# Loads of tokens in halves, and of logits, each issued once a crossbar transpose has landed

## The chip, the cores and the metric

One core of one Trainium2 chip. The metric is the device time of one execution in microseconds (us). An execution also has a span, from its first to its last instruction, which is 1.75 us shorter, and a mean granted clock of TensorE. In the profile PE is TensorE (PEld its weight loads), DVE is VectorE, ACT is ScalarE, POOL is GpSimd, SP is SyncE; a `q` behind one of them is its sequencer.

With one core there are no two dies to compare. An execution is called slow here only if it took over 1.5% more than the fastest of the same kernel.

## The reference, cut to what matters

```python
# x: (8, 4160, 192), weight_gen: (8, 4160, 8 heads, 7 taps), float32
w = softmax(weight_gen, axis=-1)                  # over the taps
out = einsum('bshk,bskhg->bshg', w, last_7_rows_of(x))   # each row and the 6 before it
x = out.reshape(33280, 192)
g = maximum(x @ w1, x @ w2)                       # 192 -> 1024
return g @ w_out                                  # 1024 -> 192
```

## The kernel before

A partition holds 260 consecutive tokens, its *columns*. They go through in batches of 16 columns, and a batch in *units* of 8 (4 at the start and the end). For each unit VectorE multiplies and adds (`mul`, `adds`), the result `y` is turned round by a crossbar transpose, a DMA issued by SyncE, and TensorE reads the transposed tile `yt`. Units are counted from 0; unit 6 is the second half of batch 1 and the second to be transposed by DMA.

```python
def load_x(b, o, n):                     # GpSimd's queue, float32 -> bfloat16 on the way
    ...
    nc.gpsimd.dma_start(out=xb_ts[b][:, (PAD + o) * D:(PAD + o + n) * D], in_=x[...])
    if b > 0 and o == 0:                 # the "halo": the last 6 rows of the batch before
        nc.gpsimd.dma_start(out=xb_ts[b][:, 0:PAD * D],
                            in_=xb_ts[b - 1][:, 16 * D:(16 + PAD) * D])

def transpose(u):
    b, o, n = UNITS[u]
    yt = pyt.tile([P, 8 // 2 * 3 * P], BF16, name="yt", tag="yt")          # 6 buffers
    nc.sync.dma_start_transpose(out=yt[...], in_=y_ts[b][:, o * D:(o + n) * D])
    yt_ts[u] = yt

def rest_of_1():
    shift(2); mul(1, 8)
    load_wg(5, nc.gpsimd)                # logits of batch 5
    load_x(3, 0, 16)                     # x of batch 3, whole
    adds(1, 8)

def extra(t):                            # beside tile t (one tile a column)
    u, k = TILES[t]; b, o, n = UNITS[u]; s = o + k
    ...
    if s == 3 and b + 2 < NB:
        if b + 5 < NB: load_wg(b + 5, nc.gpsimd)
        if b + 3 < NB: load_x(b + 3, 0, BATCHES[b + 3][1])
    if k == 2 and 6 < u + 1 < NU: transpose(u + 1)
    ...
```

There are two buffers for x and four for logits. GpSimd issues a load as soon as its buffer is free.

The softmax here doesn't subtract the row's maximum and nothing guards it: scores larger than these inputs give would overflow.

## Time and profile before

| | kernel before |
|---|---|
| time, median (range) | 434.65 us (433.38 to 434.81), 3 executions |
| profiled execution | 436.85 us, span 435.1, clock 0.992 |
| TensorE busy | 419.6 us, 96% |
| VectorE busy | 382.0 us, 88% |
| GpSimd busy | 29.9 us, 7% |

TensorE sets the time. What can be won is where it stands still. The view of all instructions on a transposed tile adds how long the transposes took:

```profile
DMA to landing us min/median/max: 3.1/4.7/18.2
```

The longest took four times the median, and it is the only one for which TensorE waited.

### The profile page before, as it was taken

What the parts mean: (1) busy time and instruction counts of PE and PEld (TensorE: products, weight loads), DVE (VectorE), ACT (ScalarE), POOL (GpSimd) and SP (SyncE); (2) the same over time, 40 slices, a digit from 0 to 9 for tenths busy, and PEclk for the clock granted to TensorE, in tenths of its full rate; (3) what the DMA queues carried; (4) which work ended last, traced back from release to release, by engine and by line L of the source; (5) the groups of instructions that cost most, each with busy time, mean ns of one, the idle gap of its engine ahead of it and who ended that gap; (6) DMA issues with size and microseconds to landing.
All of it is one profiled execution on the core that took longest, in us unless ns stands there. A gap on an engine that the chain in (4) does not pass through costs nothing.

```text
span 435.1 us, 9193 instructions
## 1 busy us (share of the span) xinstructions
PE 419.6 (96%) x4139; PEld 300.0 (69%) x4139; DVE 382.0 (88%) x176; ACT 351.5 (81%) x353; POOL 29.9 (7%) x60
## 2 busy tenths in 40 slices
PE   7999957999999999999999999999999999999996
PEld 7788844667666676666767677676776767666685
DVE  5989998599999999999999999999999999995000
ACT  5897864989798888879888988889897988877772
POOL 1510100001000000000010000000000000000000
PEclk9999997999999999999999999999999999999999
DMA  8995999439484696848397767739394836535112
GB/s 251 258 243 103 150 125 160 110 103 194 134 183 145 148 210 133 214 124 191 99 182 176 178 149 160 201 110 221 109 137 131 164 116 137 110 110 128 74 74 108
DMA packets 60295, 65.84 MB, mean 151 GB/s; under 512 B 49729, under 2 KB 50369, under 8 KB 60256
## 3 DMA queue, kind: packets, MB, share of 16 engines
q0 software_dynamic: 6256, 24.11, 26.8%
q1 hardware_dynamic: 48672, 15.59, 23.6%
q10 hardware_dynamic: 5328, 25.56, 15.1%
q8 instruction: 32, 0.52, 0.5%
q14 instruction: 7, 0.06, 0.1%
HBM read 35.96 MB, written 25.56 MB: 141 GB/s over the span
## 4 chain that ended last, share of the span: by engine, by line
PE 90%; DMA 6%; ACT 2%; SPq 1%; issue 0%
PE op_ps L281 38%; PE hd L226 26%; PE hd L236 14%; PE op_ps L271 5%; DMA yt<-y_t 4%; PE op_ps L264 2%; PE yps L197 2%; DMA xs<-in_x_dram 2%; PE hdp L226 1%; ACT rd_t L245 1%; PE hdp L236 1%; PE tp L479 1%; SPq L415 0%; PE pw L522 0%; ACT en_t L146 0%; ACT o_t L294 0%
## 5 line engine op out<-in xcount | busy, mean ns | idle before, releaser
L245 ACT ACTIVATE rd_t<-hd 128x2048 bf16<-128x2048 f32 (+1 forms) x166 | 230.9, 1445 | 41.9 <-PE hd L236 41.4
L281 PE MATMUL op_ps<-wo,rd_t 128*128 128x192 bf16 x2080 | 200.2, 246 | 0.0
L157 DVE TENSOR_TENSOR m_t<-xb_t,en_t 128x10752 bf16<-128x10752 bf16 (+1 forms) x36 | 187.3, 5206 | 6.4 <-ACT en_t L146 6.3
L281 PEld LDWEIGHTS <-rd_t 128*128 128x128 bf16 x2080 | 175.6, 98 | 9.2
L226 PE MATMUL hd<-yt,wdE 128*128 128x512 bf16 (+1 forms) x264 | 97.0, 371 | 7.6 <-DMA yt<-y_t 7.3
L226 PE MATMUL hd<-yt,wdO 128*128 128x512 bf16 (+1 forms) x264 | 96.0, 368 | 0.0
L175 DVE TENSOR_TENSOR m_t<-m_t 128x4608 bf16<-128x4608 bf16 (+1 forms) x31 | 76.9, 2480 | 1.1
L294 ACT COPY o_t<-op_ps 128x384 f32<-128x384 f32 (+1 forms) x89 | 56.1, 630 | 26.0 <-PE op_ps L281 24.0
L236 PE MATMUL hd<-yt,wdR 64*128 64x512 bf16 (+1 forms) x528 | 68.6, 369 | 0.0
L271 PE MATMUL op_ps<-w,yt 128*128 128x192 bf16 x260 | 64.0, 246 | 0.0
L176 DVE TENSOR_TENSOR m_t<-m_t 128x3072 bf16<-128x3072 bf16 (+1 forms) x31 | 52.9, 1706 | 1.1
L226 PEld LDWEIGHTS <-wdE 128*128 128x128 bf16 x288 | 28.1, 97 | 36.7 <-issue 19.5
L236 PEld LDWEIGHTS <-wdR 64*128 64x128 bf16 x576 | 20.9, 94 | 45.3 <-issue 35.6
L146 ACT ACTIVATE en_t<-wg_t 128x896 bf16<-128x896 f32 (+1 forms) x36 | 34.1, 961 | 2.1 <-ACT o_t L294 2.1
L226 PEld LDWEIGHTS <-wdO 128*128 128x128 bf16 x288 | 28.3, 98 | 10.5 <-issue 1.0
L271 PEld LDWEIGHTS <-yt 128*128 128x128 bf16 x260 | 25.4, 98 | 9.6 <-issue 0.3
L177 DVE TENSOR_TENSOR y_t<-m_t 128x1536 bf16<-128x1536 bf16 (+1 forms) x31 | 28.9, 933 | 1.1
L113 POOL DMA_DIRECT2D xb_t<-in_x_dram x19 | 10.3, 541 | 221.3 <-DVE m_t L157 221.3
L264 PE MATMUL op_ps<-w,yt 64*128 64x192 bf16 x260 | 25.2, 243 | 0.2 <-ACT o_t L294 0.2
L264 PEld LDWEIGHTS <-yt 64*128 64x128 bf16 x260 | 12.9, 94 | 14.9 <-issue 1.2
L130 DVE TENSOR_REDUCE sum_t<-e_t 128x128 f32<-128x896 f32 (+1 forms) x17 | 17.6, 1037 | 3.6 <-ACT e_t L125 3.6
L125 ACT ACTIVATE e_t<-wg_t 128x896 f32<-128x896 f32 (+1 forms) x17 | 15.7, 925 | 4.3 <-DMA wg_t<-in_weight_gen_dram 2.6
(50 smaller groups left out, 143.3 us busy)
## 6 DMA issues: line engine op xcount, KB each, us to landing
out_dram<-o_t ACTq DMA_DIRECT2D x29, 768.0 KB, 3.3
xb_t<-in_x_dram POOLq DMA_DIRECT2D x14, 768.0 KB, 7.5
wg_t<-in_weight_gen_dram POOLq DMA_DIRECT2D x14, 448.0 KB, 4.6
xb_t<-xb_t POOLq DMA_DIRECT2D x16, 288.0 KB, 7.9
out_dram<-o_t ACTq DMA_DIRECT2D x6, 384.0 KB, 5.6
wg_t<-in_weight_gen_dram SPq DMA_DIRECT2D x2, 448.0 KB, 4.9
xs<-in_x_dram SPq DMA_DIRECT2D x2, 384.0 KB, 6.6
xb_t<-in_x_dram POOLq DMA_DIRECT2D x2, 384.0 KB, 7.4
```

The source lines that it names most:

```text
L146: nc.scalar.activation(out=_sub(en_ts[b], o * WGC * 2, [[2 * N, K], [2, N], [1, 2]]), in_=_sub(wg_ts[b], o * WGC, [[1, K], [K, N], [0, 2]] ...
L157: nc.vector.tensor_tensor(out=m_ts[b][:, K * o * D:K * (o + n) * D], in0=_sub(xb_ts[b], o * D, [[D, K], [1, n * D]]), in1=_sub(en_ts[b], o ...
L175: nc.vector.tensor_tensor(out=taps(0, 1, 3), in0=taps(0, 1, 3), in1=taps(3, 1, 3), op=ALU.add)
L176: nc.vector.tensor_tensor(out=taps(0, 2, 2), in0=taps(0, 2, 2), in1=taps(1, 5, 2), op=ALU.add)
L177: nc.vector.tensor_tensor(out=y_ts[b][:, o * D:(o + w) * D], in0=taps(0, 1, 1), in1=taps(2, 1, 1), op=ALU.add)
L226: nc.tensor.matmul(hid_out(t, f, j), lhsT=wd[kind][:, f * P:(f + 1) * P], rhs=_sub(yt_ts[u], 2 * j * P, [[3 * P, w // P], [1, P]]), start= ...
L236: nc.tensor.matmul(hid_out(t, f, j), lhsT=wd["R"][r, f * P:(f + 1) * P], rhs=_sub(yt_ts[u][r, :], P, [[3 * P, w // P], [1, P]]), start=fir ...
L245: nc.scalar.activation(out=rd[:, k * 1024:(k + n) * 1024], in_=hd[:, at:at + n * 1024], func=AF.Relu)
L264: nc.tensor.matmul(op_out(c), lhsT=yt_ts[u][r, (3 * i + 1) * P:(3 * i + 2) * P], rhs=w10[r, 2 * D:3 * D], start=first, stop=False, skip_gr ...
L271: nc.tensor.matmul(op_out(c), lhsT=yt_ts[u][:, (3 * i + 2 * j) * P:(3 * i + 2 * j + 1) * P], rhs=w10[:, j * D:(j + 1) * D], start=False, s ...
L281: nc.tensor.matmul(op_out(c), lhsT=rd[:, k * 1024 + at:k * 1024 + at + P], rhs=wo[:, f * D:(f + 1) * D], start=False, stop=(f == FCH - 1), ...
L294: nc.scalar.copy(out=_sub(o_t[0], (k + 2 * q) % 24 * D, [[2 * D, w], [D, 2], [1, D]]), in_=_sub(tile_, at + q * D, [[D, w], [512, 2], [1, ...
```

## The change

Loads and transposes share the DMA engines. The intent is that a load starts only when the current transpose has landed, and is done before the next is issued. For this x comes in halves, and in front of each load GpSimd copies one element per partition out of the landed tile into a scrap tile (`gate`), so that its queue waits for the landing. This copy is called the *gate* below.

```diff
@@ transpose(u)
         yt_ts[u] = yt
+
+        c = b + 1 if o == 0 else b + 2
+        if u > 5 and c < NB:
+            nc.gpsimd.tensor_copy(out=gate, in_=yt[:, 0:1])
+            if o == 8:
+                load_x(c, 0, min(8, BATCHES[c][1]))
+            else:
+                if BATCHES[c][1] > 8:
+                    load_x(c, 8, BATCHES[c][1] - 8)
+                if b + 3 < NB:
+                    load_wg(b + 3, nc.gpsimd)
@@ rest_of_1()
         mul(1, 8)
-        load_wg(5, nc.gpsimd)
-        load_x(3, 0, 16)
         adds(1, 8)
@@ extra(t)
-        if s == 3 and b + 2 < NB:
-            if b + 5 < NB:
-                load_wg(b + 5, nc.gpsimd)
-            if b + 3 < NB:
-                load_x(b + 3, 0, BATCHES[b + 3][1])
```

## The prediction

> **What bounds the kernel now.** I read the page's busy shares first, then the waits of TensorE, then the stretch around the one long wait.
>
> ```profile
> PE 419.6 (96%) x4139; PEld 300.0 (69%) x4139; DVE 382.0 (88%) x176; ACT 351.5 (81%) x353; POOL 29.9 (7%) x60
> ...
> PE hd L226 <- DMA yt<-y_t: 7.3, 1, 7.3
> PE warm L493 <- DVE ident L431: 3.0, 1, 3.0
> PE yps L197 <- DVE m_t L157: 0.7, 1, 0.7
> ```
>
> TensorE (PE) is busy 96% of a span of 435.1 us, and all its waits but one are short or belong to the start. The exception is 7.3 us, once: the first hidden-layer matmul of a unit (half a batch, 8 columns of tokens) waits for a crossbar transpose. So the change has one stall to remove, and the rest of the span is TensorE's own work. The chain that ended last says where:
>
> ```profile
> 46.97 2.79 ACT rd_t L245 x2
> 49.76 0.20 ACT en_t L146
> 49.96 18.20 DMA yt<-y_t
> 68.17 0.05 issue
> 68.21 1.89 PE hd L226 x4
> 70.10 1.34 PE hd L236 x6
> ...
> 75.12 0.86 PE hd L226 x4
> 75.98 0.75 PE hd L236 x6
> ```
>
> The transpose of unit 6 (second half of batch 1) is issued at 49.96 and lands 18.20 us later; the median of the 31 transposes is 4.7 us. TensorE's work of before ends at 60.86. After the stall the same six-and-four matmuls take 1.89 and 1.34 us in place of 0.86 and 0.75: the clock was halved. The same in the table of stretches (columns: stretch, length, busy us of PE, PEld, DVE, ACT, POOL, granted clock, DMA share, GB/s):
>
> ```profile
> 56.00:62.00 6.00, 4.86 (x58) 4.07 (x55) 5.90 (x5) 5.16 (x6) 0.00 (x0) 1.00 1.14 75
> 62.00:68.00 6.00, 0.00 (x0) 0.00 (x0) 6.00 (x2) 0.00 (x0) 0.00 (x0) 0.70 1.11 183
> 68.00:75.00 7.00, 6.79 (x53) 4.20 (x54) 6.02 (x5) 3.63 (x3) 1.06 (x2) 0.77 0.90 159
> ```
>
> The DMA engines are full (share above 1) while only 75 GB/s move between 56 and 62 us: the transpose's 256-byte packets and others' large ones hold each other up. In flight beside it, from the issues and landings in the trace: the load of x for batch 3 (768 KB, 44.72 to 54.64), its copy of 288 KB of halo rows (45.25 to 55.89), the logits of batch 5 (448 KB, 50.96 to 66.17) and two output stores (45.70 to 57.77, 54.13 to 66.87). A transpose alone, such as the one issued at 91.94, took 3.65 us.
>
> **What the Trainium skill says.** "DMA: Bandwidth & Descriptors", section "Issuing engines are not separate DMA queues": transfers from all issuers run on the same 16 engines and interleave. The trace agrees: 18.20 us beside four transfers, 3.65 alone. "TensorE: Matmul & The Clock Gate", section "Part 1: The HAM clock gate": after an idle window of about 3.4 us the clock is halved, and as much activity restores it. The trace agrees: half clock from 64.44 to 71.27 us, 3.6 us after the idle began until 3.1 us after it ended. "SBUF — State Buffer", section "Who interferes with whom": a VectorE instruction with two SBUF inputs and a GpSimd instruction that reads SBUF exclude each other. The one such meeting in this trace fits for GpSimd: the existing gate copy runs 11.06 to 11.87, while VectorE's product ends at 11.83. VectorE's next instruction took 0.68 us, as did its twin elsewhere, so no cost to VectorE is visible.
>
> **The change part by part.** *Removed:* loads issued as soon as a buffer frees, 768 KB at once. For batch 3 that was 44.72 us, and its logits at 50.96; both leave the window of transpose 6. *Left in that window:* the two output stores. The previous transpose, beside one store of 384 KB, took 4.91 us; the one after, beside several tails, 7.67. So transpose 6 should land at 49.96 + 5 to 8 = 55 to 58 us, before TensorE runs out at 60.86. The stall vanishes: 68.21 - 60.86 = 7.35 us. With it goes the half clock: (1.89 - 0.86) + (1.34 - 0.75) = 1.62 us. Sum: 8.97 us, and the profiled span would be 426.1.
>
> *Moved:* x in halves of 384 KB, each after a landing. First half of batch 3 after transpose 6 (about 56 us), its use by VectorE's product is at about 75; second half and logits of batch 5 after transpose 7 (about 69), used at about 87. In the steady state the first half is issued some 10 us later than now (5.3 us of adds plus about 4 of transpose) and is needed some 30 us after the buffer frees; loads took 7 to 10. So no product waits for x. Logits land some 10 us or more before their exponential.
>
> *Added:* 28 copies of 128x1 on GpSimd (7% busy), and 13 more x loads of 0.53 us of GpSimd time each. None is on a chain to the end unless it hinders VectorE. If the copy must wait for VectorE's product (5.75 us), the load starts up to 7 us after the transpose was issued and its last 2 us or so meet the next transpose, issued 12.04 us after the former. Such overlaps now make 4.2 to 5.6 us in place of 3.65, which is harmless below.
>
> *What limits the gain:* VectorE (DVE) needs 24.08 us per batch of 16 columns, TensorE 24.03 (two groups of three tiles in 9.01 us). VectorE also stands still once because of the stall, 5.7 us before 80.66, since the weights it multiplies come from ScalarE, which stood behind TensorE (9.4 us). It regains that, so it moves forward by 5.8 against TensorE's 8.97: TensorE gains 3.2 us on it. The margin from landing to first use by TensorE is now mostly 5 to 8.5 us (lowest 1.5, unit 20, whose transpose took 10.2 us beside a load, logits and stores). It shrinks to some 2 to 5. The nearest margin is ScalarE's logarithm behind VectorE's sum: 3.4 to 3.9 us at batches 5, 8, 11 and 14, so 0.2 to 0.7 after. It holds, barely.
>
> *From the profile to the time:* the profiled execution took 436.85 us, the others 433.38 to 434.81 (median 434.65). If the 2.2 us between them is profiling alone, the gain is 8.97 and the time 425.7. If it is all a shorter stall without the profiler, the gain is 6.8 and the time 427.9. Midway is 426.8; I add 0.3 for a transpose or a sum that comes late somewhere. Predicted: **427.1 us**, 1.7% below.
>
> **The rivals.**
> 1. *VectorE becomes the bound.* For: it is 88% busy, gapless from 80.66 to the end of its work at 397.5, and 0.05 us per batch slower than TensorE already; 28 copies that exclude it at 0.1 us each would put it 2.8 us back, past ScalarE's margin, and TensorE would inherit some 2 us: 429. Against: the existing copy and the GpSimd issues cost it nothing visible (5.75 us each product, everywhere).
> 2. *Another transpose stalls TensorE.* Unit 7 would be used at 80.47 - 8.97 = 71.5 us and landed at 69.66 now; its neighbours change to the halved load of batch 3. If it takes 2 us longer, or a store meets load and transpose as at unit 20, TensorE stands 1 to 3 us: 428 to 430. One such stall restores the old margin, so it isn't paid many times.
> 3. *The stall isn't caused by the loads but by the stores.* Then transpose 6 would still land late. Against: at 50 to 56 us the loads' queue held 57% of the engines, the stores' 17%. If half of the excess stayed, landing at 61 to 63, the clock could hold and the gain be about 6.5 to 8: 427 to 428.
> 4. *Transposes get quicker everywhere.* It pays nothing: all others already land before use.
>
> **Range and chances.** At most 9 us can be won, and the 2% line is at 425.96, a gain of 8.7. Only the full gain without any late transpose passes it: 0.27. Slower by 2% would need the gain lost and a new cost of as much: 0.02. Eight in ten: 424.8 (full gain and a run in which the old stall was longer) to 430.5 (the stall goes, about half the gain is given back to VectorE or to a new stall).
>
> **What would show it.** Right: TensorE's wait for the transpose gone from its list, mean clock above 0.998 (0.992 now), transpose 6 landing by 58 us, no halved clock in mid-kernel, VectorE without its 5.7 us gap, GpSimd waiting for transposes instead of products. Wrong: another TensorE wait for a transpose or for ScalarE, VectorE products over 5.75 us or gaps between them of more than 0.1 us, products waiting for x.

## The result, and the profile after

427.89 us (427.68 to 428.09, 4 executions) against 434.32 us for the kernel before in the same measurement. Ratio 0.9854, 95% interval 0.9836 to 0.9873: 1.5% faster. Ratios here are the mean time of one kernel's fast executions over that of the other's in the same rounds, so not quite the ratio of the medians that are quoted.

| | before | after |
|---|---|---|
| span of the profiled execution | 435.1 us | 425.9 us |
| granted clock | 0.992 | 1.000 |
| longest transpose | 18.2 us | 7.4 us |
| transpose of unit 6: issued, landed | 49.96, 68.17 | 49.72, 53.37 |
| TensorE starts unit 6 | 68.21 | 60.46 |
| VectorE's last instruction ends | 397.5 | 391.4 |

Busy times first, then all that TensorE waited for, both of the kernel after:

```profile
PE 418.4 (98%) x4139; PEld 300.2 (70%) x4139; DVE 381.8 (90%) x176; ACT 351.5 (83%) x353; POOL 81.5 (19%) x101
```

```profile
PE warm L504 <- DVE ident L442: 3.0, 1, 3.0
PE hdp L237 <- ACT yt L214: 0.2, 1, 0.2
PE hd L237 <- ACT rd_t L256: 0.2, 1, 0.2
PE op_ps L275 <- ACT o_t L305: 0.2, 1, 0.2
```

No wait for a transpose is left, only 3.0 us at the very start and three waits of 0.2 us. The view of the transposed tiles, shown above for the kernel before, now says:

```profile
DMA to landing us min/median/max: 2.8/4.3/7.4
```

The chain that ended last runs through TensorE where it held 18.20 us of DMA, and the four and six matmuls of unit 6 take what they take everywhere:

```profile
59.96 0.66 PE op_ps L292 x8
60.62 0.86 PE hd L237 x4
61.48 0.76 PE hd L247 x6
```

The table of stretches (columns as in the prediction) shows full clock, TensorE busy, and a share of the DMA engines of 0.62 where it was 1.14, 1.11 and 0.90:

```profile
56.00:62.00 6.00, 6.00 (x65) 4.50 (x64) 5.90 (x5) 4.92 (x6) 1.27 (x3) 1.00 0.62 117
62.00:68.00 6.00, 6.00 (x61) 4.11 (x56) 6.00 (x2) 5.07 (x5) 1.82 (x1) 1.00 0.62 157
68.00:75.00 7.00, 7.00 (x65) 4.48 (x63) 6.90 (x6) 6.58 (x8) 1.32 (x3) 1.00 0.62 159
```

What the transpose's packets themselves paid stands in the view of the DMA queues (queue, packets, MB, share of 16 engines). Before, from 49.9 to 68.2 us:

```profile
q1 hardware_dynamic: 2356, 0.60, 57.8%
```

After, from 49.7 to 61 us:

```profile
q1 hardware_dynamic: 1568, 0.39, 18.2%
```

q1 is SyncE's queue, here transposes alone. A packet held an engine for 0.578 x 16 x 18.3 / 2356 = 0.072 us before and 0.182 x 16 x 11.3 / 1568 = 0.021 us after.

The 9.2 us between the two spans add up: 7.35 of wait, 1.62 of half clock, and 0.25 that unit 5's start was already earlier (45.35 against 45.10), from a start-up wait that varies. The times differ by only 6.4 us. That gap between 9.2 and 6.4 had to be explained too.

### The profile page after: what moved, and what is told of

It reads as the page before. It is cut to its first block, busy times and chain, and to the rows that moved or that the text cites. A ratio compares the mean times of both kernels' runs of the same rounds, so it can differ in the third digit from the quotient of the medians.

```text
span 425.9 us, 9277 instructions
## 1 busy us (share of the span) xinstructions
PE 418.4 (98%) x4139; PEld 300.2 (70%) x4139; DVE 381.8 (90%) x176; ACT 351.5 (83%) x353; POOL 81.5 (19%) x101
## 4 chain that ended last, share of the span: by engine, by line
PE 94%; ACT 3%; DMA 2%; SPq 1%; issue 0%
PE op_ps L292 40%; PE hd L237 27%; PE hd L247 14%; PE op_ps L282 5%; PE op_ps L275 3%; PE yps L208 2%; DMA xs<-in_x_dram 2%; PE hdp L237 1%; ACT rd_t L256 1%; PE hdp L247 1%; PE tp L490 1%; SPq L426 1%; PE pw L533 0%; ACT en_t L146 0%; ACT o_t L305 0%; ACT xb_t L455 0%
## 5 line engine op out<-in xcount | busy, mean ns | idle before, releaser
L192 POOL CAST gate<-yt 128x1 f32<-128x1 bf16 x28 | 45.8, 1635 | 278.9 <-DMA yt<-y_t 278.9
L275 PEld LDWEIGHTS <-yt 64*128 64x128 bf16 x260 | 12.8, 94 | 14.6 <-issue 0.7
```

Of the source, the lines that this page charges most:

```text
L192: nc.gpsimd.tensor_copy(out=gate, in_=yt[:, 0:1])
L275: nc.tensor.matmul(op_out(c), lhsT=yt_ts[u][r, (3 * i + 1) * P:(3 * i + 2) * P], rhs=w10[r, 2 * D:3 * D], start=first, stop=False, skip_gr ...
```

## The experiments

Each was run against the kernel before on the same chip; the three sets ran on three chips, where the medians of the kernel before were 434.99 (runs 1 to 4), 434.23 (5 to 8) and 434.90 (9 to 11). "Margin" is the time from a transpose's landing to TensorE's first use of it, from the landings and the matmuls in the trace.

By their ratios alone runs 2, 3, 4, 6 and 7 can't be told from the changed kernel: their intervals overlap its 0.9836 to 0.9873, because the kernel before varies so much. Two other things tell them apart: each of their profiles has waits for a transpose that the changed kernel's two profiles lack, and none of their 20 executions came under 429.35 us, while none of the changed kernel's eight came over 428.09 (these ran in other measurements, not beside them).

### 1. The kernel before, again

No edit.

> The kernel before, unchanged, run again. Its profiled execution had a span 9.2 us above that of the changed kernel (435.1 against 425.9), its four timed runs only 6.4 us (434.32 against 427.89). Theory 1 (the whole gain is the one wait for transpose 6 and the half clock behind it, and the length of that wait differs from execution to execution): the new profile has a wait of 4 to 6.5 us, and its span is 425.9 + 0.25 + the wait + 0.4 to 1.7 us of half clock. Rival (the extra 2.8 us of the first profile come from something spread over the kernel): the wait is again 7.3 us and the span near 433.

433.18 us (429.68 to 435.89, 4 executions), beside it seven more of the kernel before, 431.23 to 437.67. Ratio 0.9965, interval 0.9871 to 1.0059: the same kernel, as it should be. Its profile, TensorE's waits:

```profile
PE hd L226 <- DMA yt<-y_t: 4.7, 1, 4.7
```

The same unit, now 4.7 us; the transpose took 15.58. The span is 433.6, 7.7 us above 425.9: 0.25 of start, 4.7 of wait, and 2.75 left for the half clock, more than my 0.4 to 1.7. The half clock lasted the same 6.83 us as in the first profile (64.35 to 71.17), but TensorE was back at work 5.69 us before its end, not 3.06, and half of 5.69 is 2.85. So here the shorter wait saved less than its length. That is no rule: in run 5 a wait of the same length, 4.75 us, was followed by only 3.12 us of work at half clock, a loss of 1.56. Executions with a clock of 0.998 to 1.000 had spans of 427.9 to 429.4, those of 0.987 to 0.992 had 432.4 to 435.9. So the loss differs from execution to execution, and the profiled one of the first measurement was a long case. The four executions of the changed kernel differ by 0.4 us.

### 2. Only the window of unit 6 mended

```diff
 rest_of_1():
-        load_x(3, 0, 16)
 extra(t), s == 3:
+            if b == 1:
+                nc.gpsimd.tensor_copy(out=gate, in_=yt_ts[6][:, 0:1])
+                load_x(3, 0, 16)
             load_wg(b + 5, nc.gpsimd)      # batch 6
```

> The kernel before, with one change: the x load of batch 3 (whole, 768 KB) and the logits of batch 6 are issued once transpose 6 has landed; all later loads as before, none gated, none halved. Theory 1 (all of the gain lies in that one window): 427.4 to 428.4 us, no wait of TensorE for a transpose, margins of later units larger than in the changed kernel or equal. Rival (the gates and halves of the later 27 landings carry part of the gain): 429 us or more.

432.04 us (429.35 to 436.85). Ratio 0.9923, interval 0.9836 to 1.001; the profiled execution, 436.85, is a slow one. Transpose 6 landed in 3.66 us and TensorE did not wait for it. My theory that this one window held the whole gain fell: none of the four executions came under 429.35, and TensorE's list has

```profile
PE hd L226 <- DMA yt<-y_t: 7.0, 2, 6.4
```

The 6.4 us ended at 162.56 us, at unit 14. The next two runs show a wait there in fast executions.

### 3 and 4. Only x, or only logits, moved out of that window

```diff
 only x: as in 2, with load_wg (batch 6) ahead of the gate
 only logits: as in 2, with load_x(3, 0, 16) left in rest_of_1
```

> The kernel before, but only the x load of batch 3 with its halo copy waits for transpose 6; the logits of batch 6 are issued at about 51 us as before. If the x load and its halo copy are what stretches the transpose: 427.5 to 428.5 us and transpose 6 lands by 57 us. If the logits behind it are (they and the transpose crawl together from 56 to 66 us, when x and halo have landed): 432 to 434 us and transpose 6 lands after 62. If both count: between, landing 57 to 62, time within 428 to 430, as TensorE needs it at 60.9.

> The kernel before, but only the logits of batch 6 wait for transpose 6; x of batch 3 and its halo copy are issued at about 44.7 us as before. If x and halo are the cause: 432 to 434.5 us, transpose 6 lands after 63. If the logits are: 427.5 to 428.5, landing by 58. If either alone is harmless and only their sum with the stores is not: both this run and the one with only x moved come out at 427.5 to 429.

430.86 us (429.46 to 432.39), ratio 0.9917, interval 0.9842 to 0.9991; and 431.48 us (429.60 to 435.34), ratio 0.9916, interval 0.9825 to 1.0007. Transpose 6 took 5.40 us with only x moved and 7.16 with only logits moved: taking either away was enough, so neither alone makes the long transpose. In both runs the landing of transpose 6 fitted a branch of what I expected and the time did not. The lost time came back at unit 14, with a wait of 2.3 us with only x moved and of 4.0 with only logits moved. The chain of the run with only logits moved:

```profile
146.12 0.40 PE op_ps L281 x5
146.52 13.63 DMA yt<-y_t
160.15 0.04 issue
160.19 1.01 PE hd L226 x2
161.20 1.40 PE hd L236 x6
```

It is the picture of before, 97 us later. In flight beside that transpose were x of a later batch (141.37 to 149.80), logits (147.19 to 159.90) and a store (147.65 to 160.98). In the kernel before the same transfers came near unit 14, logits and store 3 us after the transpose's issue; it took 7.42 us and had 4.49 us to spare. Two things changed. The margin shrank: without the early wait TensorE runs 8.7 us earlier and VectorE, which produces `y`, only 5.6. And the meeting became worse: logits and store now came 0.7 and 1.1 us after the transpose's issue. The smaller margin alone doesn't explain the wait, since the 11.9 us from issue to use of the kernel before would not have covered 13.63 us either, nor the 16.16 us of run 2 (they would have covered the 11.45 us of run 3).

### 5. All but the window of unit 6

```diff
-        if u > 5 and c < NB:
+        if u > 7 and c < NB:
 and load_wg(5), load_x(3, 0, 16), load_wg(6) where they were before
```

> The changed kernel, but around units 6 and 7 the loads go as in the kernel before: x of batch 3 whole at about 44.7 us, logits of batch 5 at 35 and of batch 6 at 51; all landings from unit 8 on are gated. New theory (a transpose that meets a load of x, a load of logits and an output store together is stretched to 10 to 18 us, wherever that is; each of the two halves of the change removes such meetings in its own part of the kernel): the wait of 4 to 8 us at unit 6 is back with its half clock, no other wait follows, 431 to 436 us with a wide spread. Rival (the stretch at unit 6 needs the later traffic): 427.5 to 428.5.

435.13 us (434.11 to 437.39), ratio 1.0004, interval 0.994 to 1.0067. The wait at unit 6 is back, and it is the only one for a transpose:

```profile
PE hd L237 <- DMA yt<-y_t: 4.8, 1, 4.8
```

Later transposes were quick (3.6 to 5.3 us from unit 8 to 34), which gained nothing. So the mended early window is needed, and by run 2 it is not enough.

### 6. Halves without the gate

```diff
-            nc.gpsimd.tensor_copy(out=gate, in_=yt[:, 0:1])
```

> The changed kernel without the copies that make GpSimd wait for a landing: the same halves in the same order of issue, but each goes as soon as its buffer is free. If the waiting is what counts: transposes of 10 us and more are back at unit 6 or at a later unit with a small margin, 430 to 436 us. If halving and the new order suffice: 427.5 to 428.5, transposes all below 8 us.

431.70 us (430.31 to 435.25), ratio 0.993, interval 0.9857 to 1.0003. Transposes of 10.7 us (unit 8) and 14.6 us (unit 20) are each followed by a wait of TensorE, 1.66 and 3.95 us:

```profile
PE hd L236 <- DMA yt<-y_t: 5.6, 2, 4.0
```

So the gate is needed.

### 7. The gate without halves

```diff
-                load_x(c, 0, min(8, BATCHES[c][1]))
+                load_x(c, 0, BATCHES[c][1])
-                if BATCHES[c][1] > 8:
-                    load_x(c, 8, BATCHES[c][1] - 8)
```

> The changed kernel with x loaded whole: 768 KB and halo after the landing of a batch's second half, logits alone after the landing of the first half, nothing halved. If the gate with logits kept apart from x is enough: 427.5 to 428.7 us, no wait of TensorE over 0.5 us, although x's tail reaches 2 to 3 us into the next transpose. If the halves are needed: a transpose over 9 us, a wait of TensorE of 1 to 6 us, 429 to 434 us.

431.74 us (430.35 to 435.86), ratio 0.9908, interval 0.9835 to 0.9981. TensorE's waits in its profile:

```profile
PE hd L234 <- DMA yt<-y_t: 5.5, 2, 4.9
```

The 4.9 us are at unit 27: x ran from 299.75 to 307.06, the transpose was issued at 302.72, a store at 304.24, and the transpose took 14.45 us. Logits were not in flight. A whole x load, 7.3 us here, reaches the next transpose; a half, 3.8 to 5.3 us in the changed kernel, mostly does not. So the halves are needed as well.

### 8. Two output stores left out of the kernel before

```diff
-            if i % w == w - 1:
+            if i % w == w - 1 and u not in (1, 2):
```

> The kernel before without the two output stores that were in flight beside transpose 6 (wrong result on purpose: 8 columns of the output are never written). x of batch 3 and logits of batch 6 go as before. If the stores are a needed part of the meeting: transpose 6 lands by 58 us and TensorE does not wait there, but a wait comes at unit 12 or 14 as in the run with only unit 6 mended. If the loads alone suffice: transpose 6 takes 12 us or more and TensorE waits at 60.9.

Transpose 6 took 7.4 us and TensorE did not wait there, so the stores are a needed part of that meeting. Later, a transpose of 18.6 us at unit 20 cost 9.1 (I had expected the wait at unit 12 or 14). The median is 435.23 us, but two of four executions are slow ones, the profiled one, with that wait of 9.1 us, among them; the fast ones, 429.47 and 431.38, give 0.9889 with an interval of 0.98 to 0.9978.

### 9. Four gate copies in place of one

```diff
-            nc.gpsimd.tensor_copy(out=gate, in_=yt[:, 0:1])
+            for _ in range(4):
+                nc.gpsimd.tensor_copy(out=gate, in_=yt[:, 0:1])
```

> The changed kernel with four gate copies in place of one before each load. Rival 1 of the prediction (the copies hinder VectorE): products over 5.75 us or gaps between VectorE's instructions, VectorE's last instruction later than 391.4. If only GpSimd pays: VectorE unchanged. If each copy waits out one VectorE instruction (the single ones end 0.04 us after the product in 25 of 28 cases), the loads start up to 8 us later, meet the next transpose, and waits of TensorE return: 429 to 434 us. If only the first of four waits: 427.6 to 428.3.

447.56 us (434.97 to 453.82). Three of the four executions count as slow against the profiled one, so there is no ratio. First the changed kernel, GpSimd and then VectorE in order of time (start, length):

```profile
53.50 2.77 POOL L192 CAST gate<-yt 128x1 f32<-128x1 bf16 x1 [26.30 <-DMA yt<-y_t]
56.21 0.54 POOL L113 DMA_DIRECT2D xb_t<-in_x_dram  x1
```

```profile
50.47 5.75 DVE L157 TENSOR_TENSOR m_t<-xb_t,en_t 128x10752 bf16<-128x10752 bf16 x1
56.26 2.56 DVE L175 TENSOR_TENSOR m_t<-m_t 128x4608 bf16<-128x4608 bf16 x1
```

The copy starts at 53.50 and ends at 56.27, 0.04 us after VectorE's product. Of the 28 copies 27 end 0.04 to 0.05 us after the VectorE instruction under way (three of these are adds). With four copies, GpSimd:

```profile
53.56 8.14 POOL L193 CAST gate<-yt 128x1 f32<-128x1 bf16 x4 [25.70 <-DMA yt<-y_t]
61.65 0.53 POOL L113 DMA_DIRECT2D xb_t<-in_x_dram  x1
```

Each waits out one VectorE instruction, 8.14 us in all. The load then starts at 61.65, the transpose of unit 7 is issued at 61.81 and takes 15.01 us, and TensorE waits 5.8. VectorE is not slowed by the copies: its products take 5.746 to 5.758 us with 112 of them as with 28. It waits for x instead:

```profile
DVE m_t L157 <- DMA xb_t<-in_x_dram: 3.9, 1, 3.9
```

The delayed load and the returned wait were expected, at 429 to 434 us. That the three unprofiled executions took 12 to 19 us more than the median of the kernel before was not; I did not look further into them.

### 10 and 11. The gate as a small DMA, and the changed kernel again

```diff
-            nc.gpsimd.tensor_copy(out=gate, in_=yt[:, 0:1])
+            nc.gpsimd.dma_start(out=gate_d, in_=yt[0:16, 0:16])
```

> The changed kernel with the gate copy replaced by a DMA of 512 bytes out of the landed tile, which GpSimd's queue issues once the transpose has landed; nothing waits for VectorE. Theory: loads start 0.7 us after each landing instead of up to 2.9, so transposes meet less of their tails: none above 6.5 us, smallest margin of landing before first use above 2 us (1.0 in the changed kernel). The time stays 427.5 to 428.2, since TensorE waits for nothing in either. Rival (margins were not set by the loads' tails): margins as in the changed kernel.

> The changed kernel again, on whatever chip this is. All theories: 427.5 to 428.3 us with a spread under 0.6 us, clock 0.999 or 1.0 in each execution, where the kernel before spreads over 7 us.

427.77 us (427.42 to 427.97), ratio 0.9843, interval 0.9789 to 0.9898, for the DMA gate; 427.71 us (427.66 to 427.86), ratio 0.9842, interval 0.9777 to 0.9907, for the changed kernel. The kernel before took 434.90 (432.01 to 438.20) beside them. With the DMA gate x's load starts 1.1 us after each landing, against 0.6 to 2.9 us. The time is the same, as expected. The margins were not what I expected: the longest transpose still took 7.4 us and the smallest margin was 1.1 us (7.4 and 8.2, 1.0 and 0.5 in the two profiles of the changed kernel). At unit 26, where the 7.4 and the 1.1 stand, a store was issued within 0.1 us of the transpose and both loads had already landed. So that margin is set by a store, which the change does not order. Tails of loads, the parts of them that are still in flight when the next transpose is issued, have not stopped counting: the smallest margin of all, 0.5 us at unit 27 of run 11, followed a transpose of 8.2 us that had a store and the last 2.3 us of a half of x beside it.

### What all profiles say of the meetings

I sorted the 390 transposes from unit 6 on, in the 13 profiles of all kernels, by which loads and stores were in flight beside them for over 0.5 us of their first 5 us, or of less if they landed sooner (9 that met another transpose are left out). "x" is a load of x or its halo copy:

| beside it | transposes | median us | longest us |
|---|---|---|---|
| none | 104 | 3.7 | 5.3 |
| logits | 5 | 3.7 | 4.4 |
| store | 104 | 4.5 | 7.7 |
| store, logits | 10 | 4.8 | 6.1 |
| x | 25 | 4.6 | 6.2 |
| x, logits | 19 | 6.0 | 9.3 |
| store, x | 54 | 5.8 | 15.0 |
| store, x, logits | 60 | 7.4 | 18.6 |

All 13 above 10 us have both a store and an x load beside them, but most transposes with this company stay below. Of the 30 transposes in a profile, nine had it in the kernel before, three in the changed one (five in run 11). The table is an association; runs 3, 4, 7 and 8 are the tests of it. One thing it can't separate, and no run does: the halo copy always goes with a load of x, and 12 of the 13 had both beside them (the other, of 10.7 us in run 6, had a half of x without it).

## Why the prediction was right or wrong

- **Time and mechanism: right.** 427.1 predicted, 427.9 measured, within the range. The wait at unit 6 and its half clock went (8.97 us predicted, 9.2 in the spans), the clock rose above 0.998, VectorE's gap closed.
- **Landing of transpose 6:** 55 to 58 predicted, 53.37 measured. I took the stores as they were; without the loads they too are quick (2.5 us for the one issued at 45.45, 12.1 before).
- **From profile to time: the second assumption held, its reason did not.** I weighed "profiling alone" against "a shorter stall without the profiler". Neither: the stall varies by execution, profiled or not (run 1), and the first profile had a long one. A kernel without the stall needs no such correction: my span of 426.1 and the 1.75 us by which times exceed spans give 427.9, which is what was measured. That the midway figure plus 0.3 came within 0.8 us of it is in part luck.
- **Rival 4 failed, and with it the view that only unit 6 matters.** I wrote that quicker transposes elsewhere pay nothing, since all others land before use. That was true with the old margins, which the old wait had bought, and with the old order of meetings. Runs 2, 3 and 4 took the wait away at unit 6 alone and then waited at unit 14, where the margin was smaller and the transpose longer (11.5 to 16.2 us, 7.4 before). Rival 2 had this in it ("another transpose stalls"), but I gave it to the changed kernel's first units and did not see that the later gates are what keeps it off.
- **Margins:** 2 to 5 us predicted, 1.0 to 7.1 measured up to unit 34. The loss against before was as worked out: TensorE moved forward by 9.2 us at unit 9, VectorE's product for batch 3 by 6.1 (80.66 to 74.56). What I mis-sized was the transpose: 4.2 to 5.6 us predicted for one that meets a load's tail, up to 7.4 measured beside a store alone (unit 26) and 8.2 beside a store and a tail (run 11). The margin that I called the nearest, ScalarE's logarithm behind VectorE's sum at batches 5, 8, 11 and 14, came out as worked out: 0.2 to 0.7 us predicted, 0.79, 0.64, 0.49 and 0.33 measured. It is now the smallest margin that I know of in the kernel.
- **Rival 1 (VectorE hindered by the copies): out.** Products took 5.746 to 5.753 us, no gaps; run 9 with 112 copies agrees. The copy's wait for VectorE was as predicted from a single case.
- **Rival 3 (stores, not loads): half right.** Run 8 shows the stores were a needed part, runs 3 and 4 that each load was. I had argued from queue shares, which don't tell a necessary part from the rest.
- **Slips without effect:** the logits issued at 50.96 were of batch 6; those of batch 5 had been issued at 35.29, so that transpose 5 had their tail beside it and not a store alone. The "four transfers" beside transpose 6 are five in the prediction's own list.

What stays open is why these three queues hold each other up so much; the profile shows packets that take three times as long, not what they wait for. Open too is whether it is the load of x or its halo copy that counts.

## What to carry to other kernels

A stall that shows once in a long pipeline can be what gives later stages their margin and keeps their transfers apart: mended alone, it came back here at the next weak place. So ask what the margins, and the meetings of transfers, will be afterwards. Where a latency-critical DMA shares its engines with bulk transfers, order the bulk behind its landing and cut it to fit before the next; here neither half of that was enough alone. Before trusting a stall's length from one profile, look at several executions.

## What the Trainium skill lacked or had wrong

- "DMA: Bandwidth & Descriptors", section "Rules for kernel authors", says that a transpose next to ordinary DMAs needs nothing. For correctness no run here disagrees; for time, a transpose of 384 KB took 3.65 us alone, up to 15.0 us beside a store and an x load with a cast, and 18.6 with logits as well. No page I found gives that cost.
- "SBUF — State Buffer", section "Who interferes with whom", was confirmed for GpSimd's copy against VectorE's two-input instructions (27 of 28 copies ended 0.04 to 0.05 us after one). It doesn't say how copies in a row fare: here the first lost to the product under way, each of the other three started 0.07 us after VectorE's next instruction and lost to that; the four took 8.14 us, and VectorE's products took no longer (5.746 to 5.758 us).
- "TensorE: Matmul & The Clock Gate", section "Part 1: The HAM clock gate", asks for an idle window of about 3.4 us. In run 3 an idle time of 2.29 us halved the clock for 3.41 us, from 1.07 us after work had resumed; in run 6 one of 1.66 us did not. So here an idle time of two thirds of such a window (2.29 of 3.41 us) was enough, and one of half was not, each seen once.
